# An attention block and a long convolution on one core: the constants and rules of the kernel's own planner changed

## The chip, the cores and the metric

The kernel runs on one core of a Trainium2 chip. The time is device microseconds, from the start of the program to its end, the median of the runs shown. A profiled execution stands beside them; its rows give the durations that are used below. PE is the matrix engine, DVE VectorE, ACT ScalarE, POOL GpSimd, SP the queue that issues most transfers.

## The reference

Two independent computations, their results side by side in the last dimension. A is an attention block over 2048 positions, width 512, 32 heads of 16. B is a gated long convolution: a short causal filter of 4 taps over k, times v, then for each of 512 channels a causal convolution as long as the sequence, plus a direct term, times q.

```python
# A
qkv = (x @ wqkv) as (3, B, H, S, Dh);  scores = q k^T * Dh ** -0.5
p = softmax(scores);  o = p v;  a = o @ wo
# B
k_shift = sum over t of k_pad[:, t:t + S, :] * shift_k[:, ks - 1 - t]
kv = k_shift * v
y = irfft(rfft(kv padded) * rfft(ssm_k padded))[:S] + kv * ssm_D
b = q * y
out = concat([a, b], -1)
```

## The kernel before, in words

**Blocks and chunks.** The 32 heads are worked as 16 pairs of a head group `o` (128 columns of the projections, eight heads) and a block of 512 queries `qb`; each pair has two halves (even and odd heads), so there are 32 groups `n`. A group's scores are 64 blocks: 16 key tiles times 4 heads, each 128 keys by 512 queries, one PSUM bank. 2048 blocks in all. A *chunk* `T` is what one step takes: the scores of up to three (at the start four) blocks (`qk_mm`, L711), and one ScalarE exponential over their banks (`emit_exp`, L744), two chunks alternating over banks 0 to 5. The next step multiplies the exponentials of chunk T-2 with the values (`emit_pv`, L827) into bank 6 (PVB).

**VectorE's share.** Some blocks are not given to ScalarE: `dve_block` picks one of a chunk's three, and `exp_on_dve` makes its exponential of five VectorE instructions: FX from the score bank (L786), three EH steps (L793), PTD (L798). The bank is free again after FX. Such a chunk has two blocks on ScalarE and one on VectorE. `T_DVE` is the first chunk in which this is allowed. VectorE also evicts every projection and convolution result and normalises each finished group (`finish_group`: DT L888, DR, DTN, OTN).

**Units.** Between chunks PE works *units*: projections of queries ("q", L396), keys ("k", L405), values ("v", L428), the short filter ("kv", L417), the output projection ("op", L938). Each has two halves of matmuls and one eviction by VectorE (KTo L453, VA L475, KV L463, OUTA L946). A query unit is evicted to the single staging tile QS (L444), and eight small transfers, issued by POOL at L261, spread it over QT; the eviction of the next query unit waits for them. In the first 72 chunks (`N_OPEN`) units use bank 7 (BGB). Later bank 7 belongs to the convolution, and units need a *window*: one of the six score banks is held back for some chunks (`take_banks`, `hold`), so that chunks on that side have two blocks.

**The convolution.** 128 groups of four channels, called quads here (`qd` in the code). For each, four loads of 512 KB bring shifted copies of the kernel from a scratch in HBM into a ring WR of 16 tiles (`load_wr`, issued by SP); a quad's slot is refilled when its last matmul is done. `conv_lags` works 16 lags of four 128x128 matmuls a quad (L997) into bank 7. After every four quads VectorE evicts to YB (L1011); after every eight a *turn* (`conv_turn`, L1022) transposes on PE and VectorE multiplies with q in QN (L1031). Before, a turn is a job in a window.

**What sets the order.** The kernel is written for Bass, each engine's list by hand-written code at build time. Every `Eng` keeps a clock `t`, and each operation has a modelled duration; `dma` models when a transfer lands. From these the planner decides per chunk which work comes next (`emit_bg`, `unit_step`, `room`, `dve_block`). `urgent` puts an eviction on VectorE and fills the time ahead of it with background steps (`advance`), as long as they overrun the eviction's due time by no more than a slack (`S_U` for units, `S_T`, `S_C`, `S_FX`). `early` and `jobs` list units with due chunks. `warm_up` fills PE's pauses with dummy matmuls (L1202). On the chip nothing of this is decided: each engine runs its list in order and waits on semaphores. So what a wrong duration in the plan costs is a wait.

Lines that matter below: L396 to L475 units, L509 POOL's mask of the short filter (issued once its taps have landed), L711 scores, L744 exponentials, L786 to L798 VectorE's exponentials, L827 values, L997 lags.

## Time and profile before

| | us |
|---|---|
| median of the runs shown | 843.53 (843.51 to 844.29) |
| profiled execution, whole | 844.68 |
| its span | 842.9 |
| ACT busy, 728 instructions | 826.8 |
| DVE busy, 1392 instructions | 815.0 |
| PE busy, 13747 matmuls | 785.1 |
| POOL busy | 78.5 |

The chain that ended last is 88% ScalarE's exponentials (L744) and 6% VectorE. The granted TensorE clock is 0.997 of full speed over the span. A row of the trace gives the start, the duration, the engine, line and tiles of one or several equal instructions, and in brackets the engine's idle time just before it and what ended it. Successive instructions of one engine overlap a little, so the step from start to start, and not the duration, is what adds up.

### The profile page before, as it was taken

Reading aid. Unit: us, or ns where it says so; the run is one execution under the profiler, and the core shown is the slowest. Engines: PE = TensorE matmul, PEld = TensorE weight load, DVE = VectorE, ACT = ScalarE, POOL = GpSimd, SP = SyncE. Lnnn points to the kernel's source line nnn. Section 1 sums busy time; section 2 is a strip of 40 time slices with the busy share of each in tenths; the row PEclk is TensorE's granted clock in tenths of the full one; section 3 lists DMA queues with packets and bytes.
Section 4 is the critical chain, followed back from the end, with each engine's and each line's share of the span. In section 5 each row is a group of like instructions: output and inputs, shape, how many; then the busy total and the mean of one; then the engine's idle time right before and its main releaser. Section 6 shows DMA issues by size and latency. Waiting matters only on the chain.

```text
span 842.9 us, 30734 instructions
## 1 busy us (share of the span) xinstructions
PE 785.1 (93%) x13747; PEld 333.3 (40%) x13788; DVE 815.0 (97%) x1392; ACT 826.8 (98%) x728; POOL 78.5 (9%) x155
## 2 busy tenths in 40 slices
PE   8898999999999999999989999999999999999997
PEld 3343334444344444444434434434433433433442
DVE  4999999999999999999989999999999999999995
ACT  6999999999999999999989999999999999999997
POOL 3300121010100100100030010011002011000000
PEclk9999999999999999999999999999999999999999
DMA  9997199999999999999999999999999999999942
GB/s 226 218 317 276 31 371 381 406 357 357 390 401 407 377 385 377 349 388 326 345 354 383 376 366 382 363 396 398 405 408 357 408 367 409 392 358 398 363 189 76
DMA packets 109235, 291.42 MB, mean 346 GB/s; under 512 B 37680, under 2 KB 41648, under 8 KB 108720
## 3 DMA queue, kind: packets, MB, share of 16 engines
q1 hardware_dynamic: 102256, 280.80, 89.8%
q0 software_dynamic: 5648, 8.27, 3.1%
q8 instruction: 109, 1.79, 0.9%
q10 hardware_dynamic: 1200, 0.39, 0.2%
q14 instruction: 22, 0.18, 0.1%
HBM read 276.83 MB, written 6.42 MB: 336 GB/s over the span
## 4 chain that ended last, share of the span: by engine, by line
ACT 88%; DVE 6%; PE 4%; DMA 1%; issue 0%; DVEq 0%
ACT PT L744 88%; DVE EH L793 3%; PE PS L711 1%; DVE FX L786 1%; DVE PTD L798 1%; DMA QT<-QS 1%; PE PS L827 1%; PE PS L997 1%; PE PS L523 1%; DVE KTo L453 0%; DVE VA L475 0%; DVE DT L888 0%; PE PS L1202 0%; PE PS L405 0%; PE PS L396 0%
## 5 line engine op out<-in xcount | busy, mean ns | idle before, releaser
L744 ACT ACTIVATE PT<-PS 128x1536 bf16<-128x1536 f32 (+2 forms) x721 | 821.9, 1441 | 4.2 <-PE PS L711 3.7
L711 PE MATMUL PS<-QT,KTo 32*128 32x512 bf16 x2044 | 286.6, 385 | 34.4 <-ACT PT L744 6.4
L793 DVE SCALAR_TENSOR_TENSOR EH<-EH,FX 128x512 f32<-128x512 f32 x456 | 303.6, 680 | 0.1
L997 PE MATMUL PS<-WR,KV 128*16 128x128 bf16 (+15 forms) x8192 | 212.2, 220 | 1.8 <-issue 1.6
L827 PE MATMUL PS<-PT,VA 128*32 128x512 bf16 x1820 | 196.5, 390 | 4.8 <-DVE DT L888 3.3
L997 PEld LDWEIGHTS PS<-WR,KV 128*16 128x16 bf16 (+15 forms) x8192 | 144.0, 87 | 82.3 <-issue 49.0
L711 PEld LDWEIGHTS PS<-QT,KTo 32*128 32x128 bf16 x2044 | 72.4, 91 | 230.0 <-ACT PT L744 179.5
L1202 PE MATMUL PS<-IDN,ZW 128*32 128x512 bf16 (+4 forms) x640 | 161.4, 332 | 0.5 <-DVE QN L1031 0.3
L786 DVE TENSOR_SCALAR FX<-PS 128x512 f32<-128x512 f32 x228 | 155.0, 683 | 2.6 <-PE PS L711 2.6
L793 DVE SCALAR_TENSOR_TENSOR EH<-FX 128x512 f32<-128x512 uint16 x228 | 155.7, 689 | 0.1
L798 DVE SCALAR_TENSOR_TENSOR PTD<-EH,FX 128x512 uint16<-128x512 f32 x228 | 154.4, 678 | 0.1
L261 POOL DMA_DIRECT2D QT<-QS x120 | 59.7, 505 | 485.9 <-DVE QS L444 182.9
L827 PEld LDWEIGHTS PS<-PT,VA 128*32 128x32 bf16 x1820 | 47.5, 93 | 112.0 <-issue 96.0
L827 PE MATMUL PS<-PTD,VA 128*32 128x512 bf16 x228 | 68.4, 384 | 0.2 <-DVE EH L793 0.2
L1202 PEld LDWEIGHTS PS<-IDN,ZW 128*32 128x32 bf16 (+1 forms) x640 | 53.0, 96 | 26.9 <-issue 8.1
L888 DVE STREAM_TRANSPOSE DT<-PS 128x512 f32<-128x512 f32 x32 | 22.7, 710 | 6.9 <-PE PS L827 6.1
L1011 DVE CAST YB<-PS 128x512 bf16<-128x512 f32 x32 | 21.9, 685 | 1.5 <-PE PS L997 0.7
L428 PE MATMUL PS<-WKV,xT 128*128 128x128 bf16 x256 | 18.8, 220 | 1.2 <-DVE KTo L453 1.2
L405 PE MATMUL PS<-xT,WKV 128*128 128x512 bf16 (+1 forms) x51 | 15.3, 374 | 3.3 <-issue 1.4
L938 PE MATMUL PS<-WKV,OTN 128*128 128x512 bf16 x51 | 16.1, 383 | 2.2 <-issue 1.4
L396 PE MATMUL PS<-xT,WQ 128*128 128x512 bf16 x45 | 14.6, 382 | 3.3 <-issue 1.7
L827 PEld LDWEIGHTS PS<-PTD,VA 128*32 128x32 bf16 x228 | 17.0, 95 | 1.3 <-DVE EH L793 0.7
(66 smaller groups left out, 213.1 us busy)
## 6 DMA issues: line engine op xcount, KB each, us to landing
WR<-kz_scratch SPq DMA_DIRECT2D x512, 512.0 KB, 7.7
kz_scratch<-WR SPq DMA_DIRECT2D x1, 2176.0 KB, 8.2
QN<-in_B_q_dram POOLq DMA_DIRECT2D x2, 1024.0 KB, 12.5
out_dram<-QN POOLq DMA_DIRECT2D x2, 1024.0 KB, 8.8
QT<-QS POOLq DMA_DIRECT2D x120, 16.0 KB, 5.2
out_dram<-OUTA POOLq DMA_DIRECT2D x12, 128.0 KB, 5.8
QN<-in_B_ssm_k_dram SPq DMA_DIRECT2D x1, 1024.0 KB, 8.4
OTN<-in_B_ssm_k_dram SPq DMA_DIRECT2D x1, 1024.0 KB, 9.1
```

The lines of the kernel that those rows point to most:

```text
L261: f(outp, inp).then_inc(dsem.sem, 16)
L428: ins = e.matmul(PS[:, bank, 128 * j:128 * j + 128], lhsT=xT[:, dc, (4 * sc + j) * 128:(4 * sc + j + 1) * 128], rhs=WV[:, dc, o * 128:(o + ...
L711: ins = e.matmul(PS[:, bank, :], lhsT=KTo[32 * s:32 * s + 32, OF[n_] % 2, kt * 128:(kt + 1) * 128], rhs=QT[32 * s:32 * s + 32, n_ // 2 % R ...
L744: h_exp[T] = act.op(lambda e: e.activation(PT[:, p0:p0 + n, :].rearrange("p b f -> p (b f)"), PS[:, banks[0]:banks[0] + n, :].rearrange("p ...
L786: h_f = urgent(lambda e: e.tensor_scalar(fx, PS[:, bank, :], FIX_ADD, FIX_HI, ALU.add, ALU.min), [h, h_last.get(i - R_FX)], slack=S_FX)
L793: st["h"] = dve.op(lambda e: e.scalar_tensor_tensor(eh, src, (A3, A2, A1)[j], frac, ALU.add, ALU.mult), [st["h"], h_last.get(i - R_EH)], u ...
L798: lambda e: e.scalar_tensor_tensor(out16, eh, A4, fx, ALU.mult, ALU.add),
L827: ins = e.matmul(dst, lhsT=w, rhs=rhs, start=(k == 0), stop=(k == KT - 1), tile_position=(0, 32 * s))
L888: h_t = urgent(lambda e: e.transpose(out=dt, in_=PS[:, PVB, :]), [h, h_mul.get(n - 1)], slack=S_T, us=(0.63, 0.751))
L997: ins = e.matmul(PS[32 * c:32 * c + NB - n, BGB, 128 * (kk % 4):128 * (kk % 4) + 128], lhsT=KV[:, qd, n:NB, c], rhs=WR[:, r + c, 128 * (NB ...
L1011: hh = urgent(lambda e: e.tensor_copy(YB[:, half, :].rearrange("p (k i) -> p k i", k=4), src), [h, h_yb[0]], slack=S_C, us=V512)
L1202: pe.op(lambda e, s=s, k=k, rhs=rhs, bank=bank, rows=rows, c0=c0, first=first: e.matmul(PS[32 * s:32 * s + rows, bank, c0:c0 + 128 * k], l ...
```

## The change

It changes constants of the planner and some of its rules.

- *Landing times.* `dma` takes `lands`, an absolute time that replaces the modelled one, for the first loads of x and of the weights, and `after`, a least time from start to landing, set to 9.0 for the transfers out of QS.
- *Query units.* A query unit may be planned only once the modelled landing of the unit before it lies in the past. Unit 2 is planned among the early units, in bank 7.
- *Turns.* When a turn is due, a counter `bg` is set; while it stands, the convolution rests and bank 7 serves the turn, and units that are near due; no window is opened. A unit remembers the bank of its first half.
- *VectorE blocks* are allowed from chunk 2 instead of 6.
- *Constants.* Windows last 2 chunks instead of 3 with 2 between them instead of 3, `WIN_D` 1 instead of 2; slacks `S_U` 0.5 to 0.3, `S_T` 0.2 to 0.3, `S_C` 0.3 to 0.5; the convolution's pace 1.05 to 1.3, up to 8 lags a chunk instead of 6, its allowance 24 instead of 10; query units are due 24 chunks ahead instead of 12; and others below.

```diff
-LAGS = 6
-PACE = 1.05
+LAGS = 8
+PACE = 1.3
-T_DVE = 6
+T_DVE = 2
-REST = 3
-LEN = 3
-WIN_D = 2
-S_U = 0.5
+REST = 2
+LEN = 2
+WIN_D = 1
+S_U = 0.3
-S_T = 0.2
-S_C = 0.3
-PLAN = 710
-JOIN = 0.05
-JOIN2 = 0.15
+S_T = 0.3
+S_C = 0.5
+PLAN = 720
+JOIN = 0
+JOIN2 = 0.1
+Q1 = 32
+Q2 = 50
+BG_MAX = 1
+BG_NEAR = 60
-Q_DUE = 12
+Q_DUE = 24
-GAP = 8
-TAIL_GAP = 4
+GAP = 7
+TAIL_GAP = 3
-BACKLOG = 5.8
-MARGIN = 0.35
+BACKLOG = 5.2
+MARGIN = 0.4
+X_AT = ((5.6, 6.4), (9.85,), (12.5,), (14.4,))
-CAP = 10.0
+CAP = 24
...
-    def dma(eng, dsem, outp, inp, deps=(), transpose=False, kb=512, rate=DMA_KB, late=3.6):
+    def dma(eng, dsem, outp, inp, deps=(), transpose=False, kb=512, rate=DMA_KB, late=3.6, lands=0.0, after=0.0):
-        dma_t[0] = max(dma_t[0], start + late) + kb / rate
-        done[(id(h[0]), h[1])] = dma_t[0]
+        dma_t[0] = lands or max(dma_t[0], start + late) + kb / rate
+        done[(id(h[0]), h[1])] = max(dma_t[0], start + after)
...
         if u[0] == "q":
-            return u[1] < R_Q or 2 * (u[1] - R_Q) + 1 in qk_done
+            return (u[1] < 2 or 2 * u[1] - 1 in h_q and at(h_q[2 * u[1] - 1]) < pe.t) and (u[1] < R_Q or 2 * (u[1] - R_Q) + 1 in qk_done)
...
-            if held.get(b) == "w" and (part[0] or T <= win["stop"] and (T < win["begin"] + 2 or near(T, CLOSE))):
+            if held.get(b) == "w" and (part[0] and part[0][2] == b or T <= win["stop"] and (T < win["begin"] + 2 or near(T, CLOSE))):
...
+        elif state["bg"]:
+            bank, stop = BGB, 10 ** 6
         elif "bank" in win:
...
+                if state["bg"] and T >= N_OPEN and u[0] != "turn" and due - T > BG_NEAR:
+                    state["bg"] = 0
+                    return
...
         st["t"] = pe.t
+        if st["bg"]:
+            return
...
                 if st["qd"] % 4 == 0:
                     st["turn"] = st["turn"] or st["qd"] % 8 == 0
+                    if st["turn"] and not part[0] and st["qd"] < C // 4:
+                        st["bg"] = BG_MAX
                     break
```

More of the change, by code (lines that the diff above doesn't have):

```diff
@@ L311, in load_x @@
         w = 512 // parts
-        h_x[sc] = [dma(sp, d_x[sc + 4 * (i > 0)], xT[:, :, t0:t0 + w], x2[t0:t0 + w, :], transpose=True, kb=w, rate=X_KB, late=1.8)
+        h_x[sc] = [dma(sp, d_x[sc + 4 * (i > 0)], xT[:, :, t0:t0 + w], x2[t0:t0 + w, :], transpose=True, kb=w, rate=X_KB, lands=X_AT[sc][i])
                    for i, t0 in enumerate(range(sc * 512, (sc + 1) * 512, w))]
-    h_wq = [dma(act, d_w[0], WQ[:, :, 0:128], wview[:, :, 0:128], kb=128, late=1.8)]
-    h_wk = [dma(act, d_w[1], WK[:, :, 0:128], wview[:, :, D:D + 128], kb=128, late=1.8)]
+    h_wq = [dma(act, d_w[0], WQ[:, :, 0:128], wview[:, :, 0:128], kb=128, lands=3.6)]
+    h_wk = [dma(act, d_w[1], WK[:, :, 0:128], wview[:, :, D:D + 128], kb=128, lands=5.2)]
     load_x(0, 2)
-    h_wv = [dma(sp, d_w[2], WV[:, :, 0:128], wview[:, :, 2 * D:2 * D + 128], kb=128, late=1.8)]
+    h_wv = [dma(sp, d_w[2], WV[:, :, 0:128], wview[:, :, 2 * D:2 * D + 128], kb=128, lands=7.2)]
     load_x(1)
@@ L448, in evac_unit @@
                     h_q[2 * p + par] = dma(pool, d_qs[p % 2][par], QT[r0:r0 + 16, p % R_Q, par, :], QS[r0:r0 + 16, :],
-                                           [hh, h_qt0] + last, kb=16)
+                                           [hh, h_qt0] + last, kb=16, after=9.0)
         elif kind == "k":
@@ L592, in take_banks @@
             banks = list(range(ends[1], 6))
-        if T >= N_OPEN and near(T, OPEN) and T >= win.get("last", 0) + REST and "bank" not in win and len(banks) > 2 and late["bank"] is None and len(queue) > LAST_BLKS + 18:
+        if T >= N_OPEN and near(T, OPEN) and T >= win.get("last", 0) + REST and "bank" not in win and len(banks) > 2 and late["bank"] is None and len(queue) > LAST_BLKS + 18 and not state["bg"]:
             b = hold(T, banks, "w")
@@ L1040, in bass_concat_heads__mha_block__ssm_conv_h3__prompt_kernel @@
     early = [(0, ("k", 0, 0)), (0, ("v", 0, 0)), (4, ("k", 0, 1)), (6, ("k", 0, 2)), (9, ("v", 0, 1)), (11, ("k", 0, 3)),
-             (14, ("v", 0, 2)), (17, ("v", 0, 3)), (32, ("q", 1))]
+             (14, ("v", 0, 2)), (17, ("v", 0, 3)), (Q1, ("q", 1))]
     units = [("kv", c, i) for c in range(2) for i in range(4)] + [(x, 1, i) for i in range(4) for x in "kv"]
     early += [(N_OPEN - 5 - 2 * (len(units) - i), u) for i, u in enumerate(units)]
+    early = sorted(early + [(Q2, ("q", 2))], key=lambda j: j[0])
     def step(n):
         return PLAN * n // (NQB * NG)
-    jobs = [(step(2 * p) - Q_DUE, ("q", p)) for p in range(2, 16)]
+    jobs = [(step(2 * p) - Q_DUE, ("q", p)) for p in range(3, 16)]
     jobs += [(step(OF.index(o)) - 16 + 4 * sc, (x, o, sc)) for o in (2, 3) for sc in range(4) for x in "kv"]
@@ L1052, in bass_concat_heads__mha_block__ssm_conv_h3__prompt_kernel @@
     jobs.sort(key=lambda j: j[0])
-    state = {"qd": 0, "lag": 0, "turn": False, "started": False, "lags": 0.0, "left": C // 4 * NB, "t": 0.0}
+    state = {"qd": 0, "lag": 0, "turn": False, "started": False, "lags": 0.0, "left": C // 4 * NB, "t": 0.0, "bg": 0}
     part = [None]
@@ L1081, in unit_step @@
             if half:
-                due, u = part[0]
+                due, u, bank = part[0]
             else:
@@ L1096, in unit_step @@
             else:
-                ahead = (due - win["begin"] - 5) / SLOT
+                ahead = (due - (T if state["bg"] else win["begin"]) - 5) / SLOT
                 over = TURN if u[0] == "turn" else 9.0 if ahead <= 1 else press(T)
@@ L1110, in unit_step @@
                 state["turn"] = False
+                if state["bg"]:
+                    state["bg"] -= 1
+                    if not state["bg"]:
+                        return
                 continue
@@ L1115, in unit_step @@
                 (early if T < N_OPEN else jobs).remove(job)
-                part[0] = (due, u)
+                part[0] = (due, u, bank)
             if u[0] == "op":
@@ L1124, in unit_step @@
                     evac_unit(u, bank, h)
+            if half and state["bg"] and bank == BGB:
+                state["bg"] -= 1
+                if not state["bg"]:
+                    return
     def emit_bg(T):
@@ L1151, in emit_bg @@
         st["t"] = pe.t
+        if st["bg"]:
+            return
         left = min(LAGS, int(st["lags"]), int((room(T) - pe.turn("C") - SWITCH) / LAG))
```

## The prediction

> **What bounds the kernel now.** I read the profiled execution in this order: busy shares, busy time by stretch, the chain that ended last, then the rows around the few idle places. It took 844.68 us, its span is 842.9 us (1.78 us lie around the span); the median of the runs shown is 843.53 us, 1.15 us under the profiled one. All sums are made against the span and carried to the median.

> ```profile
> PE 785.1 (93%) x13747; PEld 333.3 (40%) x13788; DVE 815.0 (97%) x1392; ACT 826.8 (98%) x728; POOL 78.5 (9%) x155
> ```
> ```profile
> 200.00:300.00 100.00, 93.12 (x1802) 39.57 (x1793) 99.08 (x170) 100.00 (x87) 7.63 (x16) 1.00 1.02 393
> 400.00:500.00 100.00, 93.74 (x1661) 38.98 (x1667) 96.93 (x166) 97.47 (x88) 13.88 (x26) 0.98 0.99 367
> ```
> The second fence has stretches of 100 us; after the stretch stand the busy times of PE, PEld, DVE, ACT and POOL, then clock, DMA share and GB/s. In a normal stretch ScalarE and VectorE are both full. So there are two sums, and the longer one sets the end. The stretch from 400 us is the odd one; its loss is one place:

> ```profile
> 433.75 0.68 DVE L793 SCALAR_TENSOR_TENSOR EH<-EH,FX 128x512 f32<-128x512 f32 x1
> 436.51 0.69 DVE L444 TENSOR_SCALAR QS<-PS 128x512 bf16<-128x512 f32 x1 [2.08 <-DMA QT<-QS]
> ...
> 437.69 1.45 ACT L744 ACTIVATE PT<-PS 128x1536 bf16<-128x1536 f32 x1 [1.91 <-PE PS L711]
> ```
> A query unit's eviction (L444) waits until the eight transfers of the unit before it, 8 chunks earlier, have left the one staging tile QS. Everything behind it on VectorE waits, then the score matmuls, then ScalarE. The first transfer was issued at 426.6 us and the last landed at 436.4.

> The other place is the start:

> ```profile
> 14.88 0.69 DVE L786 TENSOR_SCALAR FX<-PS 128x512 f32<-128x512 f32 x1 [1.14 <-PE PS L711]
> ...
> 15.11 2.01 POOL L509 TENSOR_SCALAR_AFFINE_SELECT OTN<-SHK 128x2048 bf16<-128x2048 bf16 x1 [9.71 <-DMA SHK<-in_B_shift_k_dram]
> ...
> 15.60 2.06 DVE L793 SCALAR_TENSOR_TENSOR EH<-FX 128x512 f32<-128x512 uint16 x1
> ...
> 17.59 0.68 DVE L453 CAST KTo<-PS 128x512 bf16<-128x512 f32 x1
> ...
> 18.32 1.07 PE L428 MATMUL PS<-WKV,xT 128*128 128x128 bf16 x16 [1.24 <-DVE KTo L453]
> ...
> 19.76 1.45 ACT L744 ACTIVATE PT<-PS 128x1536 bf16<-128x1536 f32 x1 [0.86 <-PE PS L711]
> ```
> VectorE's share of the exponentials begins only at 14.88 us. Its second step takes 2.06 us where the same operation takes 0.68 elsewhere; it ends 0.5 us after POOL's mask (L509) does. The key eviction behind it is late, a value unit waits for that bank, and ScalarE for the matmuls queued behind the unit.

> **The change, part by part.**

> *ScalarE.* The order of the two programs gives the chunks: 370 of three blocks, 349 of two, 2 of four before; 389, 324 and none after. From start to start a chunk takes 1.330 us (three), 0.903 (two), 1.76 (four), medians of the trace, two of four alone being a mean. 19 x 1.330 - 25 x 0.903 - 2 x 1.76 = **-0.8 us**. That is all that fewer and shorter windows bring here (59 windows over 226 chunks before, 57 over 178 after; the turns of the convolution no longer need one).

> Above these medians ScalarE lost 14.9 us over the span. The query stall is 3.1 of it (2.35 at 437.69, 0.74 at 442.00). In the changed order the nearest two query units stand 20 chunks apart, at 1.15 us a chunk 23 us, against the 9.8 us that a unit's transfers took: **-3.1 us**, and nothing else waits for QS. Unit 2 moves from chunk 73 to 47, into bank 7; on POOL its eight transfers (0.48 us each) stand behind the 1.2 us issue of the QN load, whose first use is 60 chunks away, and its scores are 40 chunks away: nothing. The new rule for units is one of the planner; it adds no wait to any engine. Both halves of a unit now fall into one chunk 29 times instead of 12. Of those 12, one delayed a chunk by over 0.06 us (0.29); of some 50 split ones, eight did by 0.2 to 0.5. 17 x 0.025 - 17 x 0.05 = -0.4; I take nothing, with -0.9 and +5 (0.29 each) as ends. ScalarE's sum is **-3.9 us** plus what the start does.

> *The start.* The new landing times match the rows (x lands at 5.63, 6.52, 9.61, 12.42 and 14.33 us; the constants say 5.6, 6.4, 9.85, 12.5, 14.4). The order is now FX, EH, VA, EH, KTo, FX, EH, EH, PTD, KTo, EH, EH, FX, VA. With 0.60 us a step on VectorE (0.72 between FX and its own EH) from 9.83 us, the score matmul's end in before plus 0.06, PTD starts at 14.75 and the KTo behind it at 15.35, while POOL's mask again runs from 15.1 to 17.1, since its load is issued no earlier. If only the EH after KTo is held, to 17.66, then VA runs at 18.9, the value matmuls behind it end at 20.2 and the next scores at 20.6, for a chunk due at 19.8: 0.9 us lost, where before lost 1.05. If KTo is held as well, 0.7 more. If nothing is held, 0.9 is saved. The 2.06 row is the nearest, so I take **0**, with -0.9 and +0.6 as ends.

> [...]

> *VectorE.* From its first FX at 14.88 to its last at 821.19 us, 806.3 us, stand 1358 instructions. At back-to-back steps (0.60 for a block's five and the evictions, 0.63 for transposes, 0.33 and 0.16 for the small ones) they are 794.6 us, idle time 8.1, and 3.6 are left, 1.4 of it the long row. After, the first FX comes at 9.83, 1367 instructions follow up to the last (one block more, and two evictions now inside): 800.0 us. The last FX serves the chunk 12 before the end in both, and the tail's instructions are the same, so 21.7 us follow it. Idle: 8.1 less the 2.08 of the query wait and the 0.64 at 443.25, its echo: 5.4. Then the slacks. Those for convolution and normalising evictions grow (0.3 to 0.5, 0.2 to 0.3), and their idle rows were 2.6 and 1.0 us; at most 2.7 of that goes. That for 75 unit evictions shrinks (0.5 to 0.3): with steps of 0.6, an engine that may overrun by 0.3 instead of 0.5 idles 0.075 us on average instead of 0.008, up to 0.067 x 75 = 5, of which the same sum for the others overstates two to four times. I take them as equal, ends 2.7 and 8.1 us. 9.83 + 800.0 + 3.6 + 5.4 + 21.7 = **840.5 us of span, -2.4**; ends -5.1 and +0.3.

> VectorE's sum is the longer, so it counts: the median becomes 843.53 - 2.4 = **841.1 us**. The early blocks are worth 5.05 us of earlier start less 5.4 us of added instructions; what shortens the sum is the query wait.

> *The convolution* runs faster early: at those steps quads 8 to 64 (four loads of 512 KB each) are taken in 297 us, 5.29 us a quad; before, it was 5.7. A late quad stops PE and all behind it.

> ```profile
> GB/s 226 218 317 276 31 371 381 406 357 357 390 401 407 377 385 377 349 388 326 345 354 383 376 366 382 363 396 398 405 408 357 408 367 409 392 358 398 363 189 76
> ...
> WR<-kz_scratch SPq DMA_DIRECT2D x512, 512.0 KB, 7.7
> ```
> In before, quads that queue behind each other landed 5.13 us apart (median of 62 with no other transfer near; 5.24 mean), 5.41 with query transfers and all; every quad was there 3.1 us or more before its first use. After, quad 8 has about 4.8 us of that, so 56 quads may be 0.086 us each slower than 5.29. I cost it at 0; turns in the bank of the convolution pause it for two chunks, and the fill matmuls cover PE there (641 after, 640 before).

> **The rivals.**

> 1. *ScalarE alone counts:* VectorE's idle time falls to 2.7 us, and the end is ScalarE's: -3.9, **839.6 us**. For it: 2.6 us of idle before convolution evictions. Against: nobody reduced the PE waits behind them. Chance 0.16.

> 2. *Given back as waits:* 75 evictions with less overrun, and whole units in one chunk, leave VectorE idle 7 to 8.1 us as before: -5.05 + 5.4 + (-1.1 to 0) = -0.8 to +0.3, **843.3 us**. For it: 0.29 us at the one doubled unit that hit. Against: small single prices. Chance 0.28.

> 3. *Slower: weights land late.* Above 5.38 us a quad PE waits; for a time over the old one the stall must pass 2.4 us, that is 5.42 us. At 5.5: 56 x 0.21 - 4.8 = 7 us, **848.1 us**. For it: 5.41 with other transfers in it, and single quads at 6 to 8.8. Against: part of these were late only because issue was late. Chance 0.12. [...]

> That the change doesn't separate the query units is excluded by the order.

> **How the numbers follow.** The forecast, 841.1 (839.9 to 842.2), gets 0.44. A measurement here can tell about 0.2% from no change, 1.7 us: faster means under 841.8, slower over 845.2. Faster: 0.16 + most of 0.44 (0.40) + 0.03 of rival 2 (idle time near 6) = 0.59. Within: 0.04 + 0.25 = 0.29. Slower: 0.12. The range runs from below rival 1, where the splitting gain is added (-0.9), to the beginning of rival 3: 838.6 to 844.8.

> **What would show it.** Right: L444 no longer waits for QT<-QS and ScalarE has no gap near 1.9 us; the first FX is at 9.8; first to last FX is about 809 us; a VectorE step of some 2 us at 15.9; no PE row ended by a load of WR. Wrong: VectorE idle over 8 us between first and last FX (rival 2), ScalarE idle while VectorE has pauses (rival 1), L997 waiting for WR (rival 3).

## The result and the profile after

The changed kernel takes **851.77 us** (median of 6 runs, 848.93 to 853.63); the kernel before, run beside it, 843.91 (6 runs, 841.86 to 845.50). The ratio is **1.0087, 95% interval 1.0062 to 1.0112**: slower, where 841.1 was forecast. The profiled execution took 849.44 us with a span of 847.7 (before: 844.68 and 842.9), so the rows below show 4.8 us of the 7.9 us between the medians. One run of one kernel below (before, fast pace) was in a slower state of the chip; its median and ratio leave that run out.

Line 1 of the page of after, the busy times:

```profile
PE 779.4 (92%) x13749; PEld 333.5 (39%) x13790; DVE 817.7 (96%) x1397; ACT 827.6 (98%) x720; POOL 79.5 (9%) x155
```

Busy time by stretch, columns as in the prediction; first a stretch of before, then three of after:

```profile
100.00:200.00 100.00, 95.25 (x1824) 41.56 (x1828) 99.75 (x172) 100.00 (x91) 14.07 (x30) 1.00 0.97 359
```
```profile
100.00:200.00 100.00, 93.14 (x1900) 42.36 (x1900) 96.56 (x166) 97.68 (x86) 8.97 (x19) 0.98 0.99 378
200.00:300.00 100.00, 94.23 (x1858) 40.53 (x1855) 99.88 (x172) 100.00 (x86) 7.66 (x16) 1.00 1.03 402
...
400.00:500.00 100.00, 91.61 (x1702) 39.02 (x1704) 95.97 (x165) 97.02 (x84) 13.93 (x26) 0.98 1.00 380
```

ScalarE is as busy in all as before (827.6 against 826.8 us), so 4.0 of the added 4.8 us of span are idle time of ScalarE. It lies in a few stretches: 100 to 200 us was at 100.00 before, and 400 to 500 lost the query stall and is no fuller. From start to start, chunks took 14.9 us more than their medians before and 19.4 after.

The places that the prediction named. VectorE's query eviction, which waited 2.08 us before, in the timeline of after (no wait behind it):

```profile
433.05 0.65 DVE L449 TENSOR_SCALAR QS<-PS 128x512 bf16<-128x512 f32 x1
```

The start, in the timeline of after:

```profile
10.04 0.69 DVE L791 TENSOR_SCALAR FX<-PS 128x512 f32<-128x512 f32 x1 [0.59 <-PE PS L716]
...
15.09 2.45 POOL L514 TENSOR_SCALAR_AFFINE_SELECT OTN<-SHK 128x2048 bf16<-128x2048 bf16 x1 [9.67 <-DMA SHK<-in_B_shift_k_dram]
...
15.57 0.69 DVE L458 CAST KTo<-PS 128x512 bf16<-128x512 f32 x1
...
16.17 2.64 DVE L798 SCALAR_TENSOR_TENSOR EH<-EH,FX 128x512 f32<-128x512 f32 x2
...
19.32 0.68 DVE L480 CAST VA<-PS 128x512 bf16<-128x512 f32 x1
...
21.05 1.02 ACT L749 ACTIVATE PT<-PS 128x1024 bf16<-128x1024 f32 x1 [0.81 <-PE PS L716]
```

The key eviction passes beside POOL's mask, the two EH steps behind it take 2.64 us for two, and ScalarE's chunk at 21.05 starts 0.97 us late.

The transfers, in the page of after (slices of the span, GB/s; then the weight loads with their median time to landing, 7.7 us before):

```profile
GB/s 230 238 311 259 35 374 395 407 402 401 396 408 407 395 408 393 397 408 395 374 392 389 359 399 349 386 400 408 394 397 397 410 381 409 358 336 334 141 2 75
...
WR<-kz_scratch SPq DMA_DIRECT2D x512, 512.0 KB, 10.2
```

And what was not there before, among the waits of after (in all, times, longest; before has no row of WR):

```profile
PEld PS L1002 <- DMA WR<-kz_scratch: 6.6, 10, 1.5
...
PE PS L1002 <- DMA WR<-kz_scratch: 3.5, 4, 1.3
```

One of these waits, in the timeline of after:

```profile
380.05 0.10 PEld L1002 LDWEIGHTS PS<-WR,KV 128*16 128x16 bf16 x4 [1.51 <-DMA WR<-kz_scratch]
...
380.67 1.45 ACT L749 ACTIVATE PT<-PS 128x1536 bf16<-128x1536 f32 x1 [0.61 <-PE PS L716]
```

The convolution starts a quad, the quad has not landed, the scores stand behind it, and ScalarE waits: rival 3. But a second kind of hole is larger, and nothing in the program is waited for in it:

```profile
191.29 0.28 PE L1002 MATMUL PS<-WR,KV 128*7 128x128 bf16 x7
...
193.16 0.49 PE L1002 MATMUL PS<-WR,KV 128*6 128x128 bf16 x21 [1.59 <-issue]
...
194.03 1.45 ACT L749 ACTIVATE PT<-PS 128x1536 bf16<-128x1536 f32 x1 [0.85 <-PE PS L716]
```

A run of 28 convolution matmuls, issued together, stops for 1.59 us after the seventh. The page of the profile has a queue that could be behind it (packets, MB, share):

```profile
q8 instruction: 109, 1.79, 0.9%
```

109 transfers of 16 KB, one for each 253 records of PE and PEld in the mean (27,539 in all). In the trace one of them ended at 191.70 us, 1.46 before the 193.16 at which PE goes on. Behind holes of this kind stand 8.0 us of ScalarE's loss after (one of them, at 411.97 us, lies before score matmuls and not inside a convolution run), behind the waits for WR 1.9.

Not all of that is the hole itself. In the stretches of 2 us behind it, the third column from the right is the granted clock:

```profile
192.00:194.00 2.00, 0.83 (x28) 0.49 (x31) 0.95 (x2) 1.18 (x1) 0.00 (x0) 0.99 1.04 385
194.00:196.00 2.00, 2.00 (x35) 1.08 (x39) 1.43 (x4) 1.45 (x1) 0.00 (x0) 0.50 1.02 406
196.00:198.00 2.00, 2.00 (x44) 0.99 (x42) 1.04 (x4) 1.56 (x2) 0.00 (x0) 0.66 1.03 408
198.00:200.00 2.00, 2.00 (x38) 0.70 (x29) 2.00 (x4) 1.84 (x2) 0.00 (x0) 1.00 1.03 408
```

From 194.0 us PE has half its clock for 3.41 us; it is always busy there and still too slow for ScalarE. The same happens at 412.4 us, behind the hole at 411.97, and in before at 439.0 us, behind the query stall, whose second loss (0.74 us at 442.00) lies in it. About 2 of the 8.0 us are lost so, after the holes have ended.

### The profile page after: what moved, and what is told of

Read it like the earlier page. It is cut to its first block, busy times and chain, and to the rows that moved or that the text cites. A ratio compares the mean times of both kernels' runs of the same rounds, so it can differ in the third digit from the quotient of the medians.

```text
span 847.7 us, 30733 instructions
## 1 busy us (share of the span) xinstructions
PE 779.4 (92%) x13749; PEld 333.5 (39%) x13790; DVE 817.7 (96%) x1397; ACT 827.6 (98%) x720; POOL 79.5 (9%) x155
## 4 chain that ended last, share of the span: by engine, by line
ACT 79%; DMA 9%; PE 6%; DVE 3%; SPq 1%; issue 1%
ACT PT L749 79%; DMA WR<-kz_scratch 9%; PE PS L716 2%; PE PS L1002 1%; DVE EH L798 1%; PE PS L832 1%; SPq L266 1%; PE PS L528 1%; DVE FX L791 1%; PE PS L1225 0%; DVE PTD L803 0%; DVE DT L893 0%; PE PS L433 0%; PE PS L401 0%; DVE KTo L458 0%
## 5 line engine op out<-in xcount | busy, mean ns | idle before, releaser
L749 ACT ACTIVATE PT<-PS 128x1024 bf16<-128x1024 f32 (+1 forms) x713 | 822.7, 1454 | 8.0 <-PE PS L716 7.8
L716 PE MATMUL PS<-QT,KTo 32*128 32x512 bf16 x2044 | 282.8, 385 | 38.1 <-ACT PT L749 11.9
L798 DVE SCALAR_TENSOR_TENSOR EH<-EH,FX 128x512 f32<-128x512 f32 x458 | 306.7, 690 | 0.1
L832 PE MATMUL PS<-PT,VA 128*32 128x512 bf16 x1819 | 199.1, 391 | 6.8 <-DVE VA L480 2.5
L1002 PE MATMUL PS<-WR,KV 128*3 128x128 bf16 (+15 forms) x8192 | 197.3, 220 | 8.0 <-issue 4.0
L1002 PEld LDWEIGHTS PS<-WR,KV 128*5 128x5 bf16 (+15 forms) x8192 | 140.0, 88 | 72.9 <-issue 36.3
L791 DVE TENSOR_SCALAR FX<-PS 128x512 f32<-128x512 f32 x229 | 157.7, 690 | 6.2 <-PE PS L716 6.1
L798 DVE SCALAR_TENSOR_TENSOR EH<-FX 128x512 f32<-128x512 uint16 x229 | 155.3, 690 | 0.0
L832 PE MATMUL PS<-PTD,VA 128*32 128x512 bf16 x229 | 70.9, 385 | 0.0
L266 POOL DMA_DIRECT2D out_dram<-OUTA x12 | 6.6, 549 | 108.2 <-DVE OUTA L951 98.0
L433 PEld LDWEIGHTS PS<-WKV,xT 128*128 128x128 bf16 x256 | 14.4, 98 | 5.9 <-issue 3.9
## 6 DMA issues: line engine op xcount, KB each, us to landing
WR<-kz_scratch SPq DMA_DIRECT2D x512, 512.0 KB, 10.2
```

The source lines that it names most:

```text
L266: f(outp, inp).then_inc(dsem.sem, 16)
L433: ins = e.matmul(PS[:, bank, 128 * j:128 * j + 128], lhsT=xT[:, dc, (4 * sc + j) * 128:(4 * sc + j + 1) * 128], rhs=WV[:, dc, o * 128:(o + ...
L716: ins = e.matmul(PS[:, bank, :], lhsT=KTo[32 * s:32 * s + 32, OF[n_] % 2, kt * 128:(kt + 1) * 128], rhs=QT[32 * s:32 * s + 32, n_ // 2 % R ...
L749: h_exp[T] = act.op(lambda e: e.activation(PT[:, p0:p0 + n, :].rearrange("p b f -> p (b f)"), PS[:, banks[0]:banks[0] + n, :].rearrange("p ...
L791: h_f = urgent(lambda e: e.tensor_scalar(fx, PS[:, bank, :], FIX_ADD, FIX_HI, ALU.add, ALU.min), [h, h_last.get(i - R_FX)], slack=S_FX)
L798: st["h"] = dve.op(lambda e: e.scalar_tensor_tensor(eh, src, (A3, A2, A1)[j], frac, ALU.add, ALU.mult), [st["h"], h_last.get(i - R_EH)], u ...
```

## The experiments

Two theories. **L**: weights land late, and PE waits for them. **I**: PE's own instructions come late, by the instruction queue of the page, held up by the weight loads; at this point a supposition. The rival of both, **O**: the new order loses by itself. "Ratio" is against the kernel before on the same chip, with its 95% interval; the experiments ran in four sets, of four, four, four and three rows, in which before had medians of 845.28, 845.0, 845.83 and 844.25 us. "WR" is the number and the sum of PE's weight-load waits for WR. "Gaps" are pauses over 0.35 us, from start to start, between two convolution matmuls in a row that end 1.1 to 1.8 us after an instruction transfer's end. Both columns are counted in one profiled execution of each kernel, the medians are of 4 to 12 executions.

| kernel | median us | ratio | WR | gaps |
|---|---|---|---|---|
| before | 843.91 | 1 | none | 3, 2.3 us |
| after | 851.77 | 1.0087 (1.0062 to 1.0112) | 10, 6.6 us | 5, 5.4 us |
| after, half the weight bytes | 841.31 | 0.9961 (0.9945 to 0.9978) | none | 1, 1.0 us |
| before, half the weight bytes | 841.36 | 0.9958 (0.9943 to 0.9972) | none | 2, 0.9 us |
| after, slow pace | 841.14 | 0.9962 (0.9939 to 0.9984) | none | 3, 2.4 us |
| before, fast pace | 856.82 | 1.0167 (1.0131 to 1.0203) | none | 9, 7.9 us |
| after, split loads | 879.04 | 1.0405 (1.0381 to 1.0430) | 35, 42.5 us | 3, 2.9 us |
| after, LAGS 6 | 848.65 | 1.0041 (1.0026 to 1.0057) | 20, 13.6 us | 2, 2.6 us |
| before, query rule | 851.07 | 1.0063 (1.0045 to 1.0081) | none | 3, 2.2 us |
| after, slow pace, split | 856.23 | 1.0123 (1.0102 to 1.0144) | 30, 23.5 us | 2, 1.4 us |
| after, reads first load only | 847.48 | 1.0024 (1.0008 to 1.0040) | none | 8, 8.3 us |
| after, PACE 1.05 | 849.70 | 1.0064 (1.0041 to 1.0087) | none | 9, 10.4 us |
| after, slow pace, T_DVE 6 | 841.84 | 0.9958 (0.9943 to 0.9974) | none | 4, 3.3 us |
| after, LAGS 5 | 849.21 | 1.0046 (1.0026 to 1.0065) | 8, 6.7 us | 13, 11.5 us |
| after, CAP 10 | 844.21 | 0.9999 (0.9984 to 1.0014) | 12, 8.2 us | 3, 2.0 us |
| before, CAP 24 | 849.76 | 1.0077 (1.0050 to 1.0104) | none | 7, 7.3 us |
| after, LAGS 6, CAP 10 | 844.55 | 1.0005 (0.9992 to 1.0018) | 3, 1.9 us | 2, 1.0 us |

In the ten kernels with no wait for WR (before among them) there are 49 pauses over 0.35 us inside convolution runs, and all 49 end 1.1 to 1.8 us after an instruction transfer. Such a stretch of 0.7 us comes once in some 7.7 us, so chance would put 4 or 5 there.

**Half the bytes.** The weights' second half is left stale from quad 8 on; the order of the instructions is unchanged in both kernels.

```
+ w = S if qd < 8 else S // 2
- src = bass.AP(..., ap=[[1, 128], [1, S]]);  WR[:, 4 * i + c, :]
+ src = bass.AP(..., ap=[[1, 128], [1, w]]);  WR[:, 4 * i + c, 0:w]
```

> The changed kernel in the same order of instructions, but from quad 8 on each weight load (WR) moves half of its columns, 256 KB instead of 512 (the second half of the convolution's weights is stale, so the output of the convolution is left wrong). Theory L (weights land late and PE waits for them): all late quads go, and with them the loss; the profile names WR for 2.4 us of ScalarE's excess and the rival in the prediction had 7, so 844.5 to 849.5 us, slack above 2 us at every quad. Theory I (PE's own instructions arrive late: its gaps in the middle of convolution bursts end 1.3 to 1.5 us after a 16 KB transfer of the instruction queue; about 7 us of ScalarE's excess stand behind such gaps, 3 in the kernel before): if the fetch is slow because it queues behind the weights, the gaps shrink too and the time goes to 842 to 845; if PE merely eats its instructions too fast, the gaps stay and the time is 848 to 850. Theory O (the new order itself loses, DMA has no part): no change, 850 to 853.

> The kernel before with the same halved weight loads from quad 8 on (convolution's output wrong). No quad was late there. Theory L: no change, 843.5 to 844.5 us. Theory I with queueing behind the weights: its 3 us of excess behind fetches shrink, 841 to 842.5. Theory I by eating rate, and theory O: no change.

Theory O falls: with the transfers lighter, the same order takes 841.31 us, below every range that was put for it. The run of 28 that stopped after its seventh matmul, in the timeline of this kernel (L1003 is L1002 of after):

```profile
190.42 0.57 PE L1003 MATMUL PS<-WR,KV 128*7 128x128 bf16 x28
```

It goes through. Theory L expected nothing of the kernel before, and that too gained 0.42%, as theory I with queueing had it. Not all of this gain is shown to be instructions: between the profiled executions the gaps fell by 1.4 us, but the query wait fell too (1.22 us instead of 2.08), and 0.9 us of ScalarE's loss went at 19 us, where the loads are the same in both. The two runs of one order also show the instruction transfers starting later against PE's work: they have the same 27,539 records of PE and the same 109 instruction transfers, and at the start of a transfer PE has run 49 more records, in the mean, with full loads than with half (56 in the kernel before). That the transfer waits behind the loads meanwhile is theory I's reading of this.

**The pace.** The constants of the convolution, set back in after and put into before.

```
after:   LAGS 8 -> 6    PACE 1.3 -> 1.15   CAP 24 -> 10
before:  LAGS 6 -> 8    PACE 1.05 -> 1.3   CAP 10.0 -> 24
```

> The changed kernel with the convolution's pace set back as far as the planner still finds an order (LAGS 8 to 6, PACE 1.3 to 1.15, CAP 24 to 10): quad 64 starts at chunk 384 instead of 368, no chunk has more than 6 lags. Theories L and I both expect most of the loss to go: 841 to 845 us, no wait for WR, fewer fetch gaps. Theory O (query rule, windows, evictions, turns): 848 to 852.

> The kernel before with the new pace alone (LAGS 8, PACE 1.3, CAP 24): quad 64 starts at chunk 369 instead of 394, 193 chunks have 7 or 8 lags. Theories L and I: slower than before by 4 to 9 us, 848 to 853, with quads of slack 0 and fetch gaps as in the changed kernel. Theory O: 842 to 845.

The rest of the change at a slow pace is faster than before, as L and I had it. The pace alone makes the kernel before slower, by more than the change did and by more than either theory expected; the late quads that both expected are not there: in the profiled execution PE never waits for WR (the least slack is 0.3 us), and nine gaps are there. That execution, 852.34 us, is the fastest of this kernel, so its rows show only part of the loss; the 8 us that it lost against the profiled execution of before it lost without late weights. One gap, in its timeline (L997 is L1002 of after):

```profile
189.67 0.28 PE L997 MATMUL PS<-WR,KV 128*13 128x128 bf16 x5
...
191.02 0.57 PE L997 MATMUL PS<-WR,KV 128*12 128x128 bf16 x27 [1.06 <-issue]
```

**Split loads.** Each 512 KB load in two of 256 KB by columns, the half that is read first sent first, each with a semaphore.

```
- deps = [h_wr[qd], h_kvc[qd // 32]]
+ deps = [h_wa[qd] if n0 < NB // 2 else None, h_wr[qd] if n1 > NB // 2 else None, h_kvc[qd // 32]]
```

> The changed kernel in the same order, all its bytes moved, but each weight load is split by columns in two loads of 256 KB with a semaphore of its own each; the half that the first 8 lags read is sent first, and PE waits only for the half it reads. Each quad so has about 2.6 us more time for its first half, and the queue stays as full. Theory L (PE waits for late weights): the waits named WR go, and with them the loss, 841 to 844 us. Theory I (instructions of PE come late behind the weights): the waits named WR go, but the gaps of over 0.35 us inside convolution runs, 1.3 to 1.6 us after a 16 KB transfer of the instruction queue, stay (5 in the changed kernel, 1 with half the bytes), as does most of the loss, 846 to 850 us; if smaller rows of 2 KB instead of 4 let the instruction fetch in earlier, PE is fewer than 49 instructions later at a fetch than with half the bytes, and the gaps shrink.

> The changed kernel with the slower pace (LAGS 6, PACE 1.15, CAP 10, as in the run before that came to 841.14 us) and the split weight loads. Theory L and theory I expect no change where no quad is late, 840 to 842 us, under both kernels; by theory I it gains up to 2 us if the smaller rows let the fetches in earlier.

A miss of every theory as put, and no test between them: the split loads, with rows of 2 KB, moved more slowly. Quads that queue behind each other took 5.76 us (mean of 120) where they take 5.44 with rows of 4 KB (118), and the best slices reach 387 GB/s instead of 410. So it is a dose for L, but not a clean one: 120 x 0.32 = 38 us more of landing time made 27 us of time, and PE had half its clock for 47.8 us of the profiled execution (6.8 in after), behind pauses of up to 3.4 us; 18.7 us of ScalarE's loss lie in these stretches (2.1 in after), other waits in them included. PE was 46 records later at a fetch than with half the bytes, hardly fewer than 49.

**The parts of the pace, one at a time** (LAGS 8 to 6; PACE 1.3 to 1.05; LAGS 8 to 5), and the share of each theory.

> The changed kernel with only the burst back, LAGS 8 to 6; its pace stays (PACE 1.3, CAP 24), quad 64 starts at chunk 378 instead of 368. Theory I: fewer matmuls in a row, fewer gaps in convolution runs (1 to 3), 842 to 845 us. Theory L: the pace is what makes quads late, most of the loss stays, 846 to 850 us with quads of slack 0.

> The changed kernel with the old PACE alone (1.3 to 1.05; LAGS 8 and CAP 24 stay): quad 64 starts at chunk 383 instead of 368, but 110 chunks still have 7 or 8 lags. Theory L: hardly a late quad, 841 to 844 us, as with the slow pace and 6 lags (841.14). Theory I with the burst as what uses the instructions up: 845 to 850 us, with 4 or more gaps in convolution runs.

> The changed kernel with at most 5 lags of the convolution a chunk (LAGS 8 to 5; PACE and CAP stay), which alone holds quad 64 to chunk 384 and quad 100 to chunk 570. Theories L and I: no late quad, few gaps, 839 to 843 us, as with the slow pace.

With 6 lags there are fewer gaps (2) and more waits for WR (20), and the time is the one that L had; with the old PACE the waits go, there are more gaps (9), and the time is the one that I had. Either kernel loses 0.4 to 0.6%, so neither theory is the whole. With 5 lags both are there, against what both theories expected of it.

**The two shares.** The same loads, but PE reads and waits for the first of each four only.

```
- h_wr[qd] = dma(sp, d_wr[i], ...)
+ h = dma(sp, d_wx[i] if c else d_wr[i], ...);  (h_wx if c else h_wr)[qd] = h
- rhs=WR[:, r + c, ...]
+ rhs=WR[:, r, ...]
```

> The changed kernel in the same order and with the same loads (512 KB each, rows of 4 KB, four a quad), but PE reads only the first of the four (the convolution of the other three channels is computed from the first one's weights, so its output is wrong), and waits only for that; SP waits for the other three before it loads the place again. PE's weights so have some 3.9 us more time than in the changed kernel, whose waits for WR were 1.5 us or less, and the queue stays as full. Theory L (late weights are the loss): no wait for WR, 841 to 843 us, as with half the bytes. Theory I (late instructions are most of it): 846 to 850 us, with 4 to 6 gaps of over 0.35 us inside convolution runs 1.3 to 1.6 us after a 16 KB instruction transfer. Both, in the shares that the rows of the changed kernel give (of 11.4 us that ScalarE loses more than with half the bytes, 7.2 stand behind such gaps, 1.9 behind waits for WR): 847 to 850.

847.48 us, inside what the mixture expected and inside the range of theory I, with 8 gaps where 4 to 6 were expected; theory L by itself falls. In its timeline (L1004 is L1002 of after) the run that stopped in after, and did not with half the bytes, stops at the same matmul, with all weights there:

```profile
192.13 0.28 PE L1004 MATMUL PS<-WR,KV 128*7 128x128 bf16 x7
...
193.73 0.49 PE L1004 MATMUL PS<-WR,KV 128*6 128x128 bf16 x21 [1.32 <-issue]
```

By the medians late instructions cost 847.48 - 841.31 = 6.2 us and late weights 851.77 - 847.48 = 4.3; by the ratios to before 5.3 and 5.3, each uncertain by some 2 to 2.5 us by the intervals. About half each. "Late instructions" is here all that full loads cost when PE waits for no weight; in the profiled executions 7 us of it stand behind pauses that end shortly after an instruction transfer.

**Which constant.** CAP, the arrears that the convolution may save up while units or turns hold it back.

> The changed kernel with CAP alone back, 24 to 10 (LAGS 8 and PACE 1.3 stay): the convolution can save up at most 10 lags of arrears, so after a pause it runs ahead for a chunk or two instead of three to five. 79 chunks have 7 or 8 lags instead of 168; quad 64 starts at chunk 376. If the saved-up arrears are what makes the loss (5 lags with CAP 24 was slow, 849.21; 6 lags with CAP 10 and PACE 1.15 was fast, 841.14): 841 to 844 us. If the burst of 8 lags in a chunk is enough: 846 to 850 us.

> The kernel before with CAP alone as in the change, 10 to 24 (LAGS 6, PACE 1.05 stay): quad 64 starts at chunk 382 instead of 394. If the saved-up arrears are what makes the loss: 848 to 853 us. If it needs the burst or the pace as well: 843.5 to 846.

> The changed kernel with LAGS 6 and CAP 10, PACE 1.3 kept (the fast version had 1.15): quad 64 starts at chunk 380 instead of 384. If CAP decides, as in the fast version: 840 to 843 us. If PACE is a cause of its own (quads of slack 0): 845 to 849.

CAP alone carries most: set back in after it ends the loss (0.9999), put into before it makes 1.0077. In after LAGS 6 adds nothing to it (1.0005), and PACE 1.15 as well brings 0.9962; in before LAGS 8 and PACE 1.3 on top of it cost 0.9% more (1.0167). 844.21 and 844.55 us lie just beside the ranges that were put for them. CAP does not end the late quads: with it set back PE waits for WR 12 times, 8.2 us in all, against 10 times and 6.6 us in after, while the gaps fall from 5.4 to 2.0 us. So, as far as one profiled execution of each can tell, CAP acts through the gaps; and 8 us of waits for WR stand here in a kernel that is level with before, so the share of late weights found above is not a fixed price of a wait.

**The other steps of the prediction.**

> The kernel before with the rule for query units alone (transfers counted as 9 us, no unit before the last one's have left; Q_DUE 12 to 16, since the planner finds no order with 24). By the step of the prediction the stall of 3.1 us goes: 840.5 to 842.5 us where before is at 843.9 to 845.3, and no VectorE row waits for QT<-QS. The rival, that something else is late next there: 843.5 to 845.

> The slow version of the changed kernel (LAGS 6, PACE 1.15, CAP 10, 841.14 us) with VectorE's blocks from the seventh chunk on again (T_DVE 2 to 6). The prediction costs the early blocks at nothing (5.05 us of earlier start of VectorE against 5.4 us of instructions added): 840 to 843 us. If the early start is worth something of its own: 843 to 846.

The query rule (with Q_DUE 16) removes its stall (no wait for QT<-QS) and makes the kernel 0.63% slower, against both expectations. The planner makes another order of it; 3.5 us go at 110 us, where a value matmul waits 2.9 us for VectorE's block (L798), and more at 327 and 817; around each of the three places the clock is at half, 13.7 us in all. So this run says nothing of the rule's worth by itself. The early blocks are worth nothing: 841.84 without them, 841.14 with them, intervals overlapping.

## Why the prediction was wrong

**The step that failed is the convolution**, "I cost it at 0". It set the rate of landing against the rate of use and took the 4.8 us of room at quad 8 as enough. Two things were wrong in it, and by the runs above each cost about half of the loss.

*The size.* Of the ends 5.24 and 5.41 us a quad, the lower was taken; quads that queue took 5.44 after, and by the same count 5.42 before. By the prediction's own sum that is 56 x (5.44 - 5.38) = 3.4 us; 4.3 to 5.3 were measured. The rate of use was right: quads 8 to 64 took 5.25 us each with half the bytes (5.29 forecast). Nor is the mean over 56 quads the thing to compare: with half the bytes, where no quad is late, the 32 quads from 16 on took 5.15 us each, and at 5.44 they land 9.3 us behind that, more than the room. It takes so long a stretch: 8 quads in a row at 4.90 us are in before as well (quads 84 to 92), with no late quad. Rival 3 so had one of the two mechanisms, with 848.1 us, at too small a chance.

*What was left out.* No term stood for PE's instructions. Rows of before pointed to them: 3 gaps in convolution runs, 2.3 us, and 109 transfers of 16 KB in the instruction queue on its page. In before, after, both half-byte kernels, after at the slow pace and before at the fast pace, there are 24 pauses of this length in convolution runs; one is a wait for WR, and in each of the other 23 the matmul behind the gap comes 2.2 to 2.7 us after the instruction transfer starts, and 36 to 123 records of PE were run meanwhile. Nor did a term stand for the half clock behind a pause (3.41 us from 439.0 us on in before). By the runs above, full loads cost 5 to 6 us where PE waits for no weight; that they do so by late instructions is the author's estimate. At the start of a transfer PE was 56 records further than with half the bytes where 6 to 9 us of loads were still to land (before), and 49 where 9 to 13 were (after; the middle half of the transfers in each): more loads to land, no larger difference.

*Right:* the query stall is gone. The start is as reckoned: VA at 19.32 (18.9 forecast), the scores at 20.61 (20.6), 0.97 us lost (0.9), KTo 0.69 us long beside the mask, the two EH steps behind it 2.64. VectorE's first FX is at 10.04 (9.83). With half the bytes the sum for VectorE comes out: first to last FX 806.9 us (809), idle 4.0 in it (5.4), span 838.2 (840.5). After, idle was 12.5 us, mostly waits for scores that came late.

*Not shown:* that the order itself gains 2.4 us. With half the bytes the profiled spans differ by 2.1 us (838.2 and 840.3), but the medians are equal (841.31 and 841.36); that 841.31 lies beside the forecast of 841.1 is therefore luck. The slow version beats before by 0.2 to 0.6% and the change by some 10 us; it is the best found, level with the one with T_DVE 6.

*Open:* why 5 lags a chunk still gave 13 gaps. No run told which instructions a transfer brings. That the instruction transfers are late because of the weight loads, and that PE stands still for them, is inferred from the half-byte runs and from where the pauses end, and was not tried apart from the loads. No run separates a pause from the half clock behind it: the mean granted clock was 0.998 to 0.999 in the executions with half the bytes, 0.996 in those of before beside them and 0.997 in those of after, and in the 32 executions of before in the third set the time was 0.64 us longer for each 0.001 of clock less.

## What to carry to other kernels

A transfer that had room on average was late here where its consumer ran fast for long: compare the rate at which queued loads land with the consumer over a stretch long enough to use up the room (here 32 quads, 5.44 against 5.15 us), not over all of them. Keep small the arrears that a planner may make up at once. With DMA engines nearly always busy (a share of 0.99 to 1.03 in after's stretches of 100 us from 100 to 700 us), dense runs of small matmuls also paused with no releaser shortly after a packet of the instruction queue (in the ten kernels with no wait for WR all 49 pauses over 0.35 us ended 1.1 to 1.8 us after one); look for such pauses, and look at the granted clock behind each. A stall that is removed gives nothing if its time is spent on making another engine's demand burstier.
